# Moving three MLP pieces into a hand-written order list, with one copy moved to GpSimd

## The chip, the cores and the metric

The kernel runs on one core of a Trainium2 chip. The metric is the device time of one execution in microseconds (us), read as the median of several runs. The engines are called PE (matrix products), PEld (loading of weights for PE), DVE (the vector engine), ACT (the scalar engine), POOL (GpSimd) and SP (the engine that issues most transfers). The profiled executions are some 2 us shorter than the timed ones of the same kernel (605.9 us against 607.9). Profiles are therefore compared with profiles and times with times.

## The reference

Eight batches of attention with RMS-normalized queries and keys, then an MLP on a layer norm of the result, with a residual:

```python
q_n, k_n = rmsnorm(q, g_q), rmsnorm(k, g_k)        # q, k, v: (8, 12, 448, 64)
attn = softmax(q_n @ k_n.T / 8)
x = (attn @ v) transposed to (8, 448, 768)
xn = (x - mean(x)) / sqrt(var(x) + 1e-6) * g_ln
out = x + relu(xn @ w_ch1) @ w_ch2                 # w_ch1: 768 x 3072, w_ch2: 3072 x 768
```
(shortened; the softmax and norms are the usual ones)

## The kernel before

The twelve heads of a batch are six pairs. A "unit" is one or two pairs whose queries and keys are normalized together. Batch 0 is emitted in an order written by hand, one token for each piece of work; from then on, the MLP of one batch is interleaved with the attention of the next by arithmetic. The tokens that matter here:

- `S6.0`: scores of pair 6, key block 0, with its exponential on ACT. `V6.0`: its product with the values. `K7`, `Q7`: transposes of the keys and queries of pair 7 on PE, each emptied by a copy on DVE.
- For unit 5: `a5 c5` squares (ACT), `d5 e5` sums (DVE), `g5` root (ACT), `i5 j5` scaling and rounding of the keys (POOL), `k5 l5` two-input operations (DVE), `m5` the doubling of the queries (a copy), `z5` casts of the values (POOL).
- `A N0 N1 N2`: layer norm (DVE), `X0 X1 X2` its transposes, `U0 U1 U2`: the first three of the 24 up products of the MLP, a third of the columns at a time.

```python
POOL_DUP = (1, 2, 4)
ORDER = """
...
V5.3 V5.4 V5.5 Q6 a5 i5 V5.6 T3 T4 S6.0 S6.1 S6.2 S6.3 T5 S6.4 A V6.0 V6.1 N0 V6.2 N1 V6.3
S6.5 S6.6 d5 V6.4 X0 X1 U0 N2 R Q7 X2 c5 e5 j5 g5 k5 l5 z5 U1 U2 V6.5 M m5 V6.6 L7 K7
"""
UP_FIRST = 3
...
def scores(self, p, i):                       # two score banks rotate
    ps = self.ps_s.tile([128, 512], FP32, tag="psS", name="psS")
    nc.tensor.matmul(ps[:, 0:S], c["main"][:, ts(i, 128)], q[:, ts(h, S)], ...)
    nc.scalar.activation(out=c["E"][:, i], in_=ps[:, 0:S], func=AFT.Exp, ...)
...
def mlp_chunks(self, b):                      # a piece: 6 matmuls, and for up products a ReLU on ACT
    def up(f):
        ps = self.ps_m.tile([128, 512], FP32, tag="mlp", name="psH")   # three banks rotate
        ...
        nc.scalar.activation(out=hT[:, f, 0:N], in_=ps[:, 0:N], func=AFT.Relu)
    for f in range(0 if b else UP_FIRST, NFF):
        yield 6 * N / 2.4, (lambda f=f: up(f))
    ...                                       # then the down products, four pieces for each tile
```

The dealer walks through the pieces and, behind each, emits as many "steps" of the next batch's attention as the share of pieces done asks for. A step holds one block of scores, some values, and a part of a unit's preparation. The weights of the second MLP product are loaded in the first such step.

```python
tail = 13
chunks = list(self.mlp_chunks(b))
total = sum(c for c, _ in chunks)
start, goal = self.pos, mark[b + 1]
for i, (cost, emit) in enumerate(chunks):
    ...
    emit()
    done += cost
    upto(int(min(goal, start + (goal - start) * done / (total - 960 * tail))))
```

In batch 0, 44 steps are to be dealt. There are 45 pieces (21 up, 24 down) and the last 13 get none, so 44 steps go over 32 pieces: 1.375 steps a piece.

Of the kernel before, what the change touches and what calls it, by code (L numbers as in the profile page):

```python
# [25 lines left out]
UNIT_PAIR = [PAIR_UNIT.index((u, 0)) for u in range(len(UNITS))]  # L26
EXP_BIAS = -4.0
WARM = 22
DVE_KG, POOL_HI, POOL_DUP, ACT_Q = (0, 1), (1, 2, 3, 4, 5), (1, 2, 4), (0, 1)



# [1 line left out]


ORDER = """
b0 a0 c0 L4 i0 j0 e0 k0 gq0 l0 b1 m0 a1 c1 K0 Q0 d0 G gk0 S0.0 S0.1 d1 e1 L5 i1 g1 j1 l1 k1 m1
z0 b2 a2 S0.2 d2 c2 S0.3 S0.4 K1 V0.0 e2 i2 S0.5 Q1 g2 l2 S0.6 S1.0 j2 V0.1 S1.1 S1.2 m2 b3
V0.2 a3 V0.3 k2 c3 S1.3 K2 V0.4 S1.4 z2 V0.5 Q2 S1.5 V0.6 V1.0 i3 W0 d3 e3 S1.6 V1.1 V1.2 S2.0
j3 T0 V1.3 S2.1 S2.2 Q3 V1.4 S2.3 K3 S2.4 V1.5 V1.6 S2.5 g3 z3 S2.6 V2.0 S3.0 S3.1 V2.1 k3  # L40
S3.2 b4 S3.3 V2.2 l3 a4 V2.3 m3 S3.4 V2.4 K4 S3.5 Q4 V2.5 V2.6 S3.6 Q5 S4.0 V3.0 S4.1 V3.1 i4
V3.2 d4 T1 K5 V3.3 W1 c4 V3.4 V3.5 S4.2 S4.3 V3.6 S4.4 S4.5 W2 e4 V4.0 V4.1 j4 S4.6 S5.0 k4
S5.1 g4 V4.2 l4 S5.2 V4.3 V4.4 V4.5 S5.3 K6 V4.6 z4 V5.0 S5.4 m4 b5 V5.1 G2 S5.5 L6 V5.2 S5.6
V5.3 V5.4 V5.5 Q6 a5 i5 V5.6 T3 T4 S6.0 S6.1 S6.2 S6.3 T5 S6.4 A V6.0 V6.1 N0 V6.2 N1 V6.3
S6.5 S6.6 d5 V6.4 X0 X1 U0 N2 R Q7 X2 c5 e5 j5 g5 k5 l5 z5 U1 U2 V6.5 M m5 V6.6 L7 K7
""".split()
DMA_UNIT = 8
PE_SET = (DMA_UNIT + 1) % 2
# [27 lines left out]
class _Fast:  # L76


    def __init__(self, ctx, tc, sh, q, k, v, gs, g_ln, w1, w2, out):
        self.gs, self.g_ln = gs, g_ln  # L80
        self.tc, self.nc, self.sh = tc, tc.nc, sh
        self.q, self.k, self.v, self.w1, self.w2, self.out = q, k, v, w1, w2, out
        nc = tc.nc
        pool = lambda name, bufs, **kw: ctx.enter_context(tc.tile_pool(name=name, bufs=bufs, **kw))
        self.p_in = pool("p_in", 2)
        self.p_n = pool("p_n", 2)
        self.p_e = pool("p_e", 2)
        self.p_x = pool("p_x", 2)
        self.p_xl = pool("p_xl", 2)
        self.p_m = pool("p_m", 1)  # L90
        self.fix = pool("fix", 1)
        self.ps_tr = pool("ps_tr", 1, space=PSUM)
        self.ps_s = pool("ps_s", 2, space=PSUM)
        self.ps_o = pool("ps_o", 1, space=PSUM)
        self.ps_m = pool("ps_m", 3, space=PSUM)
        fix = self.fix
        self.kU = [fix.tile([128, 1920], FP16, name=f"kU{i}", tag=f"kU{i}") for i in range(2)]
        self.qU = [fix.tile([128, 2, 2, S], FP16, name=f"qU{i}", tag=f"qU{i}") for i in range(2)]
        self.v16 = fix.tile([128, 6, 2, 3, D + 1], FP16, name="v16", tag="v16")
        self.vl = fix.tile([128, 6, 2, D + 1], FP16, name="vl", tag="vl")  # L100
        nc.vector.memset(self.v16[:, :, :, :, D], 1.0)
        nc.vector.memset(self.vl, 0.0)
        nc.vector.memset(self.vl[0:64, :, 0, D], 1.0)
        nc.vector.memset(self.vl[64:128, :, 1, D], 1.0)
        self.rec = fix.tile([128, B * NPAIR, 4, 2], FP32, name="rec_all", tag="rec_all")
        nc.vector.memset(self.rec, 0.01)
        self.rr = fix.tile([128, 7 * B * NPAIR], FP32, name="rr_all", tag="rr_all")
        self.rs = fix.tile([128, B, 4], FP32, name="rs_all", tag="rs_all")
        nc.vector.memset(self.rs, RS_LO)
        self.hT = fix.tile([128, NFF, 512], FP16, name="hT", tag="hT")  # L110
        self.tr = self.ps_tr.tile([128, 1024], FP16, name="tr", tag="tr")
        nc.vector.memset(self.tr[:, 64:128].bitcast(FP32), 0.0)
        self.zero_left(DMA_UNIT)
        self.xs, self.xls, self.st = {}, {}, {}
        self.units, self.loads, self.prs = {}, {}, {}
        self.late, self.preps = [], {}

    def zero_left(self, u):

# [293 lines left out]
    def first_attention(self):  # L413
        nc, gln = self.nc, self.sh.gln
        self.batch(0)
        self.load_first()
        nc.scalar.add_instruction(mybir.InstLoadActFuncSet(
            name=nc.get_next_instruction_name(), act_func_set_id=LN_EXP_SET))
        nc.scalar.activation(self.sh.warm, self.sh.ones, AFT.Ln)
        ln = {}  # L420
        for x in ORDER:
            key, n = x[0], x[1:]
            if x == "S6.0":
                self.batch(1)
            if key == "L":
                self.load_unit(int(n))
            elif x == "G":
                nc.sync.dma_start(gln, self.g_ln.unsqueeze(0).broadcast_to([128, DM]))
            elif x == "G2":
                nc.gpsimd.tensor_scalar(out=gln, in0=gln, scalar1=XS, scalar2=None, op0=ALU.mult)  # L430
            elif key == "W":
                c = int(n)
                self.load_w1(1024 * c, 1024 * c + 1024) if c < 3 else self.load_w2(c - 3)
            elif key in "SV":
                (self.scores if key == "S" else self.values)(*map(int, n.split(".")))
            elif key in "KQT":
                dict(K=self.trans_k, Q=self.trans_q, T=self.stats)[key](int(n))
            elif key in "ANXR":
                ln = ln or self.ln_ops(0)
                ln[x]()  # L440
            elif key == "M":
                gmax = self.sh.gmax
                nc.vector.tensor_reduce(out=gmax, in_=self.sh.gprod, axis=AX.X, op=ALU.max,
                                        apply_absolute_value=True)
                nc.vector.tensor_scalar(out=gmax, in0=gmax, scalar1=1.0 / K_MAX, scalar2=None,
                                        op0=ALU.mult)
            elif key == "U":
                self.up_first(int(n))
            elif key == "H":
                ps = self.ps_m.tile([128, 512], FP32, tag="mlp", name="psW")  # L450
                for _ in range(int(n)):
                    nc.tensor.matmul(ps[:, 0:384], self.sh.id16,
                                     self.v16.rearrange("p s h j d -> p (s h j d)")[:, 0:384],
                                     start=True, stop=True)
            else:
                self.prep_ops(int(x[-1]))[x[:-1]]()
# [228 lines left out]
    def upto(self, target):  # L685
        while self.pos < min(target, len(self.steps)):
            for call in self.steps[self.pos]:
                call()
            self.pos += 1
# [8 lines left out]
    def run_rest(self):  # L698
        steps, mark, upto = self.steps, self.mark, self.upto
        tail = 13  # L700
        for b in range(B):
            chunks = list(self.mlp_chunks(b))
            total = sum(c for c, _ in chunks)
            if b + 1 == B:
                for i, (_, emit) in enumerate(chunks):
                    emit()
                    if i == 2:
                        self.flag()
                break
            start, goal = self.pos, mark[b + 1]  # L710
            done, items = 0.0, None
            for i, (cost, emit) in enumerate(chunks):
                if items and len(chunks) - i <= len(items):
                    items.pop(0)()
# [3 lines that stand above are left out]
                if self.pos >= goal and items is None:  # L718
                    items = self.ln_list(b + 1)
                    items.pop(0)()  # L720
            for op in items:
                op()
            if b + 2 == B:
                upto(len(steps))
# [212 lines left out]
```

## Time and profile before

| | |
|---|---|
| time, median of 3 | 607.91 us (607.86 to 608.15) |
| PE busy | 578.3 of 605.9 us |
| first score | 11.27 us |
| first layer norm transpose (X0) | 49.73 us |
| list and three dealt pieces done, first dealt score (S7.0) | 60.93 us |
| first up product of batch 1 | 121.18 us |

The last rows are milestones read off the PE instructions in order of time. A change in the order list can act only before the last of them: from there to the end, PE is full and takes the same time in every kernel of this study (484.6 to 485.0 us). In the views below, a row of stages has the stretch and its length, then the busy us and number of instructions of PE, PEld, DVE, ACT and POOL, then the granted PE clock and two columns on transfers. A row in order of time has start, duration, engine, line, operation, output from input and, in brackets, the idle time before it and what ended it. Line numbers move by three between the kernels.

### The profile page before, as it was taken

The numbers are of one execution on the slowest core, as the hardware profiler recorded it, in microseconds if no ns is written. First come the engines' busy times: TensorE is split into PE (matmuls) and PEld (weight loads), VectorE is DVE, ScalarE is ACT, GpSimd is POOL, SyncE is SP. The second block draws the span as 40 slices with busy tenths as digits, with TensorE's granted clock in tenths as the row PEclk, the third lists the DMA queues.
The fourth block names the chain that finished last, engine by engine and source line by source line (L and its number), as shares of the span: only waits on it lengthen the run. The fifth ranks groups of instructions, "written<-read, shape, count | busy, mean of one in ns | idle before, by whom it ended". The sixth has DMA issues, their size and how long they took to land.

```text
span 605.9 us, 11525 instructions
## 1 busy us (share of the span) xinstructions
PE 578.3 (95%) x4500; PEld 344.6 (57%) x4500; DVE 286.5 (47%) x618; ACT 360.7 (60%) x697; POOL 189.5 (31%) x245
## 2 busy tenths in 40 slices
PE   2877999999999999999999999999999999999995
PEld 1555666655566666655566666655566666654564
DVE  5799567734346256715256255734256322540011
ACT  6996986278752697358753598548754477124200
POOL 3853432233551355332542345423512000000000
PEclk9999999999999999999999999999999999999998
DMA  9999999479864586844944585847722330130011
GB/s 208 266 213 217 215 224 178 123 195 87 143 157 117 98 129 146 177 135 83 150 121 113 123 125 128 197 116 121 133 65 70 92 62 2 34 98 0 1 53 57
DMA packets 130861, 75.29 MB, mean 124 GB/s; under 512 B 96656, under 2 KB 121040, under 8 KB 130800
## 3 DMA queue, kind: packets, MB, share of 16 engines
q1 hardware_dynamic: 114048, 45.12, 38.3%
q0 software_dynamic: 16080, 28.94, 21.6%
q8 instruction: 37, 0.61, 0.4%
q10 hardware_dynamic: 672, 0.43, 0.2%
q14 instruction: 24, 0.20, 0.1%
HBM read 52.36 MB, written 11.01 MB: 105 GB/s over the span
## 4 chain that ended last, share of the span: by engine, by line
PE 88%; DVE 1%; ACT 1%; issue 0%
PE psC L637 36%; PE psH L621 34%; PE psS L352 8%; PE oA L381 5%; PE oB L383 2%; PE psS L356 1%; PE psS L355 1%; PE tr L330 0%; PE tr L316 0%; ACT E L358 0%; DVE x L398 0%; DVE qn L67 0%; DVE khl L240 0%; ACT khl L215 0%; ACT hT L623 0%
## 5 line engine op out<-in xcount | busy, mean ns | idle before, releaser
L621 PE MATMUL psH<-xnT,w 128*128 128x512 f16 (+1 forms) x1134 | 241.9, 353 | 0.0
L358 ACT ACTIVATE E<-psS,rr_all 128x448 f16<-128x448 f32 x336 | 207.0, 634 | 48.3 <-PE psS L352 43.0
L637 PE MATMUL psC<-w,hT 128*128 128x384 f16 (+1 forms) x1368 | 234.7, 323 | 0.0
L623 ACT ACTIVATE hT<-psH 128x512 f16<-128x512 f32 (+1 forms) x189 | 104.0, 550 | 123.9 <-PE psH L621 121.9
L637 PEld LDWEIGHTS <-hT 128*128 128x128 f16 x1368 | 127.5, 98 | 74.6
L621 PEld LDWEIGHTS <-w 128*128 128x128 f16 x1134 | 102.5, 98 | 80.9 <-issue 0.3
L352 PE MATMUL psS<-qU,kU 128*128 128x448 f16 x288 | 100.6, 357 | 8.3 <-ACT E L358 6.0
L381 PEld LDWEIGHTS <-E 128*128 128x128 f16 x1008 | 70.7, 98 | 49.1 <-issue 4.4
L229 POOL TENSOR_TENSOR qkv<-qkv,gprod 128x896 f32<-128x896 f32 x21 | 43.7, 2081 | 95.8 <-issue 49.5
L381 PE MATMUL oA<-v,E 128*128 128x65 f16 x864 | 66.7, 194 | 0.1
L641 DVE SCALAR_TENSOR_TENSOR x<-psC,rs_all,x 128x384 f32<-128x384 f32 x48 | 29.0, 616 | 71.5 <-PE psC L637 71.1
L396 DVE RECIPROCAL rec_all<-oA 128x6 f32<-128x6 f32 x48 | 9.3, 194 | 94.4 <-PE oA L381 94.2
L383 PE MATMUL oB<-v,E 128*128 128x65 f16 x288 | 51.9, 194 | 0.1
L127 POOL DMA_DIRECT2D qkv<-in_k_dram x14 | 11.2, 798 | 129.7 <-DVE qn L279 61.8
L218 DVE TENSOR_REDUCE ssq<-khl 128x14 f32<-128x896 f32 (+1 forms) x24 | 25.6, 1065 | 44.6 <-ACT khl L215 44.5
L352 PEld LDWEIGHTS <-kU 128*128 128x128 f16 x288 | 28.0, 98 | 25.5 <-issue 6.0
L218 DVE TENSOR_REDUCE ssq<-qn 128x14 f32<-128x896 f32 (+1 forms) x25 | 26.2, 1047 | 21.8 <-ACT qn L215 21.7
L67 DVE SCALAR_TENSOR_TENSOR qn<-qkv,rq 128x256 f16<-128x256 f32 (+1 forms) x72 | 26.3, 425 | 15.1 <-ACT rq L223 15.0
L383 PEld LDWEIGHTS <-E 128*128 128x128 f16 x336 | 32.5, 97 | 0.3 <-DVE xl L403 0.2
L240 DVE TENSOR_TENSOR khl<-qkv,khl 128x896 f16<-128x896 f32 x21 | 22.8, 1088 | 10.8 <-ACT khl L237 7.1
L398 DVE TENSOR_TENSOR x<-oA,rec_all 128x384 f32<-128x384 f32 x48 | 26.8, 558 | 1.5
L545 DVE BATCH_NORM_STATS2 stat<-x 128x6 f32<-128x256 f32 (+1 forms) x75 | 26.2, 404 | 0.6
(104 smaller groups left out, 447.7 us busy)
## 6 DMA issues: line engine op xcount, KB each, us to landing
out_dram<-x SPq DMA_DIRECT2D x20, 384.0 KB, 2.5
qkv<-in_k_dram POOLq DMA_DIRECT2D x14, 384.0 KB, 3.9
qkv<-in_q_dram POOLq DMA_DIRECT2D x14, 384.0 KB, 5.2
qkv<-in_v_dram POOLq DMA_DIRECT2D x14, 384.0 KB, 6.6
w<-in_moe_w_ch_dram POOLq DMA_DIRECT2D x3, 1536.0 KB, 14.6
w<-in_moe_w_ch_dram POOLq DMA_DIRECT2D x2, 2304.0 KB, 24.3
qkv<-in_k_dram SPq DMA_DIRECT2D x7, 384.0 KB, 5.7
qkv<-in_q_dram SPq DMA_DIRECT2D x7, 384.0 KB, 4.6
```

The source lines that it names most:

```text
L67: nc.vector.scalar_tensor_tensor(out=out, in0=x, scalar=8.0, in1=r.unsqueeze(2).broadcast_to([x.shape[0], g, D]), op0=ALU.mult, op1=ALU.mult)
L218: nc.vector.tensor_reduce(out=c["ssq"][:, n], in_=c["sq", n], axis=AX.X, op=ALU.add)
L229: (nc.vector if u in DVE_KG else nc.gpsimd).tensor_tensor(out=c["t"][1], in0=c["t"][1], in1=sh.gprod.unsqueeze(1).broadcast_to([128, g, D] ...
L352: nc.tensor.matmul(ps[:, 0:S], c["main"][:, ts(i, 128)], q[:, ts(h, S)], start=True, stop=True)
L358: nc.scalar.activation(out=c["E"][:, i], in_=ps[:, 0:S], func=AFT.Exp, scale=self.rr[:, g:g + 1], bias=EXP_BIAS)
L381: nc.tensor.matmul(oA[:, t, cs], E[:, i, ts(t, 128)], rhs, start=(i == 0 and t == 0), stop=(i == 6 and t == 2))
L383: nc.tensor.matmul(oB[:, cs], E[:, i, 320:448], rhs, start=(i == 0), stop=(i == 6))
L398: nc.vector.tensor_tensor(out=x[:, :, 128 * hp:128 * hp + 128].rearrange("p t (e d) -> p t e d", e=2), in0=oA[:, :, :, 0:D], in1=rec[:, 0: ...
L621: nc.tensor.matmul(ps[:, 0:N], sh.w1[:, dc, ts(f, 128)], xnT[:, dc, 0:N], start=(dc == 0), stop=(dc == NDC - 1))
L623: nc.scalar.activation(out=hT[:, f, 0:N], in_=ps[:, 0:N], func=AFT.Relu)
L637: nc.tensor.matmul(ps[:, 0:g[1]], hT[:, f, ts(t, 128)], sh.w2[:, f, cols], start=(f == 0), stop=(f == NFF - 1))
L641: nc.vector.scalar_tensor_tensor(out=x[:, cols], in0=ps[:, 0:g[1]], scalar=self.rs[:, b, t:t + 1], in1=x[:, cols], op0=ALU.mult, op1=ALU.add)
```

## The change

The intent: less waiting of PE at the end of the list. Three MLP pieces, which the dealer used to emit, now stand in the list between the last values of pair 6 and the end of unit 5's preparation, to fill PE while DVE finishes K7. Q6 and Q7 go earlier, X2 is freed from Q7, and `m5` leaves DVE for POOL.

```diff
-DVE_KG, POOL_HI, POOL_DUP, ACT_Q = (0, 1), (1, 2, 3, 4, 5), (1, 2, 4), (0, 1)
+DVE_KG, POOL_HI, POOL_DUP, ACT_Q = (0, 1), (1, 2, 3, 4, 5), (1, 2, 4, 5), (0, 1)
 ORDER = """
 ... (the earlier lines are reordered too; cut)
-V5.3 V5.4 V5.5 Q6 a5 i5 V5.6 T3 T4 S6.0 S6.1 S6.2 S6.3 T5 S6.4 A V6.0 V6.1 N0 V6.2 N1 V6.3
-S6.5 S6.6 d5 V6.4 X0 X1 U0 N2 R Q7 X2 c5 e5 j5 g5 k5 l5 z5 U1 U2 V6.5 M m5 V6.6 L7 K7
+S5.6 Q6 V5.3 V5.4 V5.5 a5 V5.6 Q7 S6.0 T4 S6.1 T3 V6.0 S6.2 i5 S6.3 T5 S6.4 A V6.1 N0 N1 V6.2
+N2 V6.3 S6.5 S6.6 d5 V6.4 X0 X1 U0 X2 c5 e5 g5 j5 l5 z5 U1 U2 C k5 V6.5 V6.6 C M R K7 m5 L7 C
 """
...
+            elif key == "C":
+                self.chunks = self.chunks or self.mlp_chunks(0)
+                next(self.chunks)[1]()
...
-            chunks = list(self.mlp_chunks(b))
+            chunks = list(self.mlp_chunks(b) if b else self.chunks)
```

The last line: the pieces that the list has taken are gone from the dealer's list, so its `total` is smaller.

More of the change, by code (lines that the diff above doesn't have):

```diff
@@ L28 @@
 WARM = 22
-DVE_KG, POOL_HI, POOL_DUP, ACT_Q = (0, 1), (1, 2, 3, 4, 5), (1, 2, 4), (0, 1)
+DVE_KG, POOL_HI, POOL_DUP, ACT_Q = (0, 1), (1, 2, 3, 4, 5), (1, 2, 4, 5), (0, 1)
 ORDER = """
-b0 a0 c0 L4 i0 j0 e0 k0 gq0 l0 b1 m0 a1 c1 K0 Q0 d0 G gk0 S0.0 S0.1 d1 e1 L5 i1 g1 j1 l1 k1 m1
-z0 b2 a2 S0.2 d2 c2 S0.3 S0.4 K1 V0.0 e2 i2 S0.5 Q1 g2 l2 S0.6 S1.0 j2 V0.1 S1.1 S1.2 m2 b3
-V0.2 a3 V0.3 k2 c3 S1.3 K2 V0.4 S1.4 z2 V0.5 Q2 S1.5 V0.6 V1.0 i3 W0 d3 e3 S1.6 V1.1 V1.2 S2.0
-j3 T0 V1.3 S2.1 S2.2 Q3 V1.4 S2.3 K3 S2.4 V1.5 V1.6 S2.5 g3 z3 S2.6 V2.0 S3.0 S3.1 V2.1 k3
-S3.2 b4 S3.3 V2.2 l3 a4 V2.3 m3 S3.4 V2.4 K4 S3.5 Q4 V2.5 V2.6 S3.6 Q5 S4.0 V3.0 S4.1 V3.1 i4
-V3.2 d4 T1 K5 V3.3 W1 c4 V3.4 V3.5 S4.2 S4.3 V3.6 S4.4 S4.5 W2 e4 V4.0 V4.1 j4 S4.6 S5.0 k4
-S5.1 g4 V4.2 l4 S5.2 V4.3 V4.4 V4.5 S5.3 K6 V4.6 z4 V5.0 S5.4 m4 b5 V5.1 G2 S5.5 L6 V5.2 S5.6
-V5.3 V5.4 V5.5 Q6 a5 i5 V5.6 T3 T4 S6.0 S6.1 S6.2 S6.3 T5 S6.4 A V6.0 V6.1 N0 V6.2 N1 V6.3
-S6.5 S6.6 d5 V6.4 X0 X1 U0 N2 R Q7 X2 c5 e5 j5 g5 k5 l5 z5 U1 U2 V6.5 M m5 V6.6 L7 K7
+b0 L4 a0 i0 c0 j0 e0 k0 gq0 l0 m0 b1 c1 d0 G a1 K0 Q0 d1 gk0 e1 L5 i1 g1 S0.0 j1 l1 z0 k1 S0.1
+m1 b2 a2 S0.2 d2 V0.0 c2 S0.3 K1 e2 S0.4 i2 Q1 S0.5 g2 l2 S0.6 V0.1 j2 S1.0 V0.2 S1.1 S1.2 b3
+m2 V0.3 k2 z2 c3 V0.4 S1.3 K2 S1.4 a3 S1.5 i3 V0.5 Q2 V0.6 V1.0 V1.1 d3 e3 S1.6 V1.2 S2.0 W0
+V1.3 S2.1 Q3 V1.4 S2.2 K3 S2.3 j3 V1.5 S2.4 g3 T0 V1.6 S2.5 V2.0 S2.6 S3.0 S3.1 z3 V2.1 k3
+S3.2 b4 S3.3 a4 i4 l3 V2.2 V2.3 m3 S3.4 V2.4 K4 S3.5 Q4 V2.5 V2.6 S3.6 V3.0 c4 V3.1 Q5 S4.0
+S4.1 V3.2 d4 V3.3 T1 W1 K5 W2 V3.4 j4 S4.2 S4.3 V3.5 V3.6 S4.4 S4.5 S4.6 e4 V4.0 V4.1 S5.0
+S5.1 k4 g4 V4.2 S5.2 l4 V4.3 V4.4 V4.5 S5.3 K6 V4.6 z4 V5.0 S5.4 S5.5 m4 L6 b5 V5.1 G2 V5.2
+S5.6 Q6 V5.3 V5.4 V5.5 a5 V5.6 Q7 S6.0 T4 S6.1 T3 V6.0 S6.2 i5 S6.3 T5 S6.4 A V6.1 N0 N1 V6.2
+N2 V6.3 S6.5 S6.6 d5 V6.4 X0 X1 U0 X2 c5 e5 g5 j5 l5 z5 U1 U2 C k5 V6.5 V6.6 C M R K7 m5 L7 C
 """.split()
@@ L115, in __init__ @@
         self.units, self.loads, self.prs = {}, {}, {}
-        self.late, self.preps = [], {}
+        self.late, self.preps, self.chunks = [], {}, None
     def zero_left(self, u):
```

## The prediction

> **What bounds the kernel now.** I read the page first (TensorE, PE, is busy 578.3 us of a 605.9 us span, so all its idle time is 27.6 us), then the busy time of each engine by stage, cut where the hand-written order list (attention of batch 0 and its layer norm, up to about 61 us) ends and where the rest begins. Columns: stretch, its length, then busy us (instructions) of PE, weight loads, DVE, ACT, POOL.
>
> ```profile
> 0.00:12.00 12.00, 2.52 (x16) 1.69 (x17) 7.05 (x20) 6.11 (x13) 3.30 (x10) 1.00 0.85 200
> 12.00:45.00 33.00, 25.59 (x299) 16.52 (x298) 27.95 (x50) 31.27 (x62) 22.20 (x26) 1.00 1.05 240
> 45.00:61.00 16.00, 11.96 (x142) 8.43 (x141) 14.60 (x36) 11.09 (x25) 6.55 (x7) 1.00 0.99 220
> 61.00:109.00 48.00, 47.83 (x450) 31.53 (x451) 30.79 (x58) 39.34 (x77) 15.77 (x15) 1.00 1.12 197
> 109.00:595.00 486.00, 485.76 (x3547) 282.24 (x3546) 204.66 (x454) 272.85 (x523) 141.70 (x190) 1.00 0.52 106
> ```
>
> From 61 us to 595 us PE has 0.4 us of idle time. So the time is: the moment at which PE becomes solid, plus PE work that no order changes. From 12 to 45 us ACT is busy 31.3 of 33 us, and DVE has almost no gap after 24 us: those two are the pace, not PE. From 45 to 61 us DVE is busy 14.6 of 16 us and PE waits 4 us. The change can act only there: 4 us in the last stage, a little in the first two.
>
> Then the PE instructions of that last stage, in order of time (start, duration, operation; in brackets the idle time before it and what ended it):
>
> ```profile
> 49.73 0.34 PE L600 MATMUL tr<-id,xn 128*128 128x128 f16 x3 [0.44 <-DVE xn L566]
> 51.19 0.51 PE L600 MATMUL psX<-id,xn 128*128 128x128 f16 x6 [0.59 <-DVE xn L566]
> 54.26 0.49 PE L600 MATMUL tr<-id,xn 128*128 128x128 f16 x6 [0.79 <-DVE qU L335]
> 54.59 2.17 PE L667 MATMUL psU<-xnT,w 128*128 128x128 f16 x36
> 57.38 3.08 PE L621 MATMUL psH<-xnT,w 128*128 128x384 f16 x18
> 60.93 0.55 PE L352 MATMUL psS<-qU,kU 128*128 128x448 f16 x2 [0.46 <-DVE kU L318]
> ```
>
> The third line is the one to see: the last layer norm transpose (X2) uses the one transpose bank that Q7 used just before, so it waits for DVE to empty Q7 (0.79 us), although its own input was ready. The last line: after three MLP pieces (18 matmuls, 3.08 us) PE waits 0.46 us for K7's evacuation. That evacuation stands at the end of a full DVE queue:
>
> ```profile
> 46.54 2.24 DVE L545 BATCH_NORM_STATS2 stat<-x 128x6 f32<-128x256 f32 x9
> 52.05 1.01 DVE L566 SCALAR_TENSOR_TENSOR xn<-x,stat,gln 128x768 f16<-128x768 f32 x1
> 53.58 0.62 DVE L335 COPY qU<-tr 128x896 f16<-128x896 f16 x1 [0.52 <-PE tr L330]
> 54.79 0.56 DVE L608 COPY xnT<-tr 128x768 f16<-128x768 f16 x1 [0.59 <-PE tr L600]
> 55.27 1.08 DVE L218 TENSOR_REDUCE ssq<-qn 128x14 f32<-128x896 f32 x1
> 58.58 0.38 DVE L279 COPY qn<-qn 128x896 f16<-128x896 f16 x1
> 60.21 0.66 DVE L318 COPY kU<-tr 128x960 f16<-128x960 f16 x1
> ```
>
> On ACT, the evacuations of the first three up products stand behind unit 5's root, which waits for a DVE sum:
>
> ```profile
> 56.38 0.23 ACT L221 ACTIVATE rt<-ssq 128x28 f32<-128x28 f32 x1 [2.65 <-DVE ssq L218]
> 56.86 1.23 ACT L671 ACTIVATE hT<-psU 128x384 f16<-128x384 f32 x3
> ```
>
> **What the Trainium skill says.** "Perfetto Trace Analysis", section "Optimization Strategy", says that kernels have regimes with different most-contended engines and that interleaving them may help. The trace agrees that there are such regimes (ACT and DVE before 61 us, PE after). The same page, section "Matmuls", wants independent matmul groups to rotate through PSUM banks so that emptying one overlaps the next; here three banks rotate, and moving a piece ahead means asking when its bank is free. "GPSIMD Engine Reference", section "4.1 Engine selection", calls one-input elementwise work on GpSimd roughly line rate. The trace differs:
>
> ```profile
> L279 DVE COPY qn<-qn x22: 291/394/395, 9.0 to 480.9; 128x896 f16<-128x896 f16 x21, 128x448 f16<-128x448 f16 x1
> L279 POOL COPY qn<-qn x3: 887/931/1661, 14.1 to 42.6; 128x896 f16<-128x896 f16 x2, 128x448 f16<-128x448 f16 x1
> ```
>
> The doubling of a whole unit takes 0.39 us on DVE and 0.93 or 1.66 us on GpSimd. "SBUF — State Buffer", section "Who interferes with whom", explains two sizes: GpSimd shares a port pair with DVE and the later one blocks. The 1.66 us copy, at 20.6 us, lay beside a two-input DVE subtraction (k2); the 0.93 us one, at 42.6 us, began as another was ending.
>
> **The change part by part.** I compared the old and new list engine by engine. No work is added or dropped on PE, ACT or DVE except that m5 leaves DVE for GpSimd; the rest is order.
>
> (1) Q6 goes before V5.3 and Q7 behind V5.6, out of the layer norm stage. DVE can then empty Q6 at about 44.4 us instead of idling 0.30 us until 44.68; so the evacuation of V5.6 starts about 0.3 us earlier, at 44.9 us, and ends at 46.25. Q7's copy (0.54 us from start to next start) is now in front of the statistics: they run 46.8 to 48.95, the aggregate to 49.35, the three norms (about 1.0 us each) to 50.35, 51.3 and 52.3. d5 (1.0 us) now follows the last norm, to 53.3. So the first transpose comes some 0.2 us later than before, the second at 51.35 (51.19 before), the third norm 0.75 us earlier (52.3 against 53.06).
>
> (2) PE: X1 51.35 to 51.7; U0's first 12 matmuls to 52.35; its last 6 wait for the bank of X1 until about 52.65, as they did (0.22 us before). X2 runs at 53.0 instead of 54.26, with Q7's 0.4 us of PE work gone into an earlier gap. Its copy on DVE 53.5 to 54.05. U1 and U2 (2 x 1.0 us) end at 55.35, where they ended at 56.6.
>
> (3) The MLP pieces now follow directly: C. But the first needs the bank of the first up product, whose evacuation stands on ACT behind g5, which needs e5 on DVE: 54.05 to 55.05, root to 55.6, evacuation to 56.05. PE waits about 0.7 us: a new wait. Then piece 56.1 to 57.05, V6.5 and V6.6 (0.35), piece to 58.4, K7 (0.4), piece to 59.8.
>
> (4) K7's wait (0.46 us). DVE: l5 from 55.5 (0.45 us of waiting for the root that k5 filled before), k5 to 57.5, V6.6's evacuation (1.3) and M (0.3) to 59.2, K7's copy to 59.8. The rest of the program is dealt out by shares of the pieces left; with three fewer left, working the program's step arithmetic by hand gives two further pieces before S7.0 (about 61.8 us), so K7 is in time and the wait is gone.
>
> (5) m5 on GpSimd: 0.30 us less DVE work before K7, 0.9 to 1.7 us on an engine that has 9 idle us in that stage; ready by 58.5 us, needed by Q8 after 65 us. Worth nothing alone.
>
> At the same amount of PE work before stood at 60.93 us and the new order stands at 59.8: a gain of 1.1 us. (6) At the start, c1 goes ahead of a1 although unit 1's q lands after its k: ACT waited 0.23 us for q at 9.67; now a1 (0.58) waits behind it, and Q0's copy comes about 0.45 us later; g1 now precedes S0.0, so l1 comes about 0.9 us earlier. By S0.3 I find ACT 0.2 us behind, and g2, which paces DVE, at 19.0 instead of 18.9. After that DVE is full with the same work, so I carry 0.1 us. Sum: -1.1 + 0.1, and 0.1 for the risk below: -0.9 us.
>
> **The rivals.** (a) A late transfer. The first half of the second MLP weights is loaded in the first dealt-out step, behind a6 on ACT and a multiplication on GpSimd. It was issued at 62.04 us:
>
> ```profile
> w<-in_moe_w_ch_dram POOLq DMA_DIRECT2D x1, 2304.0 KB, 23.4
> ```
>
> so it landed near 85.4, and the first down product began at 90.2. Now that step comes after the sixth piece instead of the third: a6 near 61.5, issue near 64.4, landing near 87.8 (an estimate, with the same 23.4 us). The down products should start near 88.7. Margin 0.9 instead of 4.8 us. If the queue is slower, PE waits up to 1.5 us and the gain is eaten: about 608. (b) DVE takes it back: Q7's copy before the statistics and the new wait for g5 grow, and only the 0.46 us go: 607.4. Speaks for it: DVE is 91% busy there. Against: the order gives 0.75 us on the third norm by plain subtraction. (c) The early reordering is worth more than I find: ACT waits 1.0 us and DVE 4 us between 12 and 24 us; if half of that were won, 605.9. Against: ACT's own work from 5.9 to 44.5 us leaves 2.3 us of gaps in all, and the new start adds one.
>
> **Range and chances.** 607.91 - 0.9 = 607.0 us. Range 605.8 to 608.1: below, (c) and a full 1.1; above, (a). 2% is 12 us; all idle time before 61 us is 21 us, of which 8.5 is the first load, so faster by 2% gets 0.01, slower 0.01, within 2% 0.98.
>
> **What would show it.** Right: X2 without a wait for Q7; a wait of 0.4 to 1 us at the first moved piece, ended by ACT; no wait for K7; S7.0 after five pieces; m5 at 0.9 to 1.7 us on GpSimd; PE solid from about 57 us; the first stages within 0.4 us of before at V5.6. Wrong: idle PE before the first down product near 89 us (a); norms ending later than 53 us (b); V5.6 over 0.6 us earlier or later (c).

## The result and the profile after

| | before | after |
|---|---|---|
| median of 6 runs each, same rounds | 608.07 us (607.86 to 609.48) | 608.95 us (608.59 to 609.14) |
| profiled span | 605.9 us | 607.2 us |
| first score | 11.27 | 11.70 |
| first score to X0 | 38.46 | 38.94 |
| X0 to first up product of batch 1 | 71.45 | 71.93 |
| rest | 484.72 | 484.63 |

The ratio of the two is 1.001, with a 95% interval of 0.9997 to 1.0023: the same within 2%, and rather slower than faster. A ratio here is the mean time of one kernel's fast runs over the mean of the other's fast runs of the same rounds, so it is not quite the ratio of the medians. The predicted 607.0 us and the range to 608.1 us were missed on the high side.

The stages of the changed kernel, as in the prediction's first view:

```profile
12.00:45.00 33.00, 25.77 (x296) 16.69 (x294) 27.51 (x50) 30.72 (x62) 22.22 (x26) 1.00 1.07 240
45.00:61.00 16.00, 12.58 (x150) 8.87 (x147) 14.62 (x34) 10.54 (x24) 7.06 (x7) 1.00 0.95 211
61.00:109.00 48.00, 46.80 (x436) 30.62 (x434) 30.11 (x56) 39.52 (x78) 15.64 (x14) 1.00 1.08 196
109.00:595.00 486.00, 485.76 (x3553) 282.82 (x3552) 205.84 (x456) 274.22 (x525) 143.04 (x190) 1.00 0.52 106
```

From 45 to 61 us PE is busy 12.58 us instead of 11.96: the change did there what it was made for. The third row is the surprise. PE was busy for 47.83 of these 48 us; now it is 46.80. Its instructions in order of time, some rows picked, show both:

```profile
53.83 0.50 PE L603 MATMUL tr<-id,xn 128*128 128x128 f16 x6
...
57.02 1.14 PE L624 MATMUL psH<-xnT,w 128*128 128x384 f16 x6 [0.68 <-ACT hT L674]
...
62.63 0.35 PE L352 MATMUL psS<-qU,kU 128*128 128x448 f16 x1
...
65.89 0.35 PE L352 MATMUL psS<-qU,kU 128*128 128x448 f16 x1 [0.17 <-ACT E L358]
...
67.63 0.35 PE L352 MATMUL psS<-qU,kU 128*128 128x448 f16 x1 [0.42 <-ACT E L358]
...
79.81 0.35 PE L352 MATMUL psS<-qU,kU 128*128 128x448 f16 x1 [0.46 <-ACT E L358]
```

X2 no longer waits, the first moved piece waits 0.68 us for its bank, and S7.0 follows without a wait: as predicted. The last three lines are new. A score waits until an exponential has emptied one of the two score banks. Before, the whole stretch from 61 us on had one such wait, of 0.2 us.

The brackets understate the loss, because the ends of matmuls are modelled. Taken from start to start, less the usual spacing of such matmuls, the breaks between 61 and 110 us are 0.33, 0.57 and 0.16 us near 66 to 70 us, 0.62 us at 79.81, and 0.24 us twice at 83.4 and 84.0: some 2 us, where the page's busy time shows 1.2. In the kernel before there are two breaks over 0.15 us in the same count: 0.63 us at K7 and 0.34 us at 66.04. One of the breaks after is not ACT's: the one at 84.0 us stands before a transpose of queries, and DVE had emptied K from the transpose bank only at 83.95 us.

A second reading needs no such sum. Before, PE had done the list and three pieces when S7.0 began at 60.93 us; 60.25 us later came the first up product of batch 1. After, the same PE work, the list with its three pieces, was done at 60.68 us (two more pieces follow before S7.0), and the first up product of batch 1 came 61.89 us later. So the list ended 0.25 us earlier, and 1.64 us were lost behind it.

Why ACT holds PE there shows in ACT's own order. Before:

```profile
58.94 0.94 ACT L215 ACTIVATE khl<-qkv 128x896 f32<-128x896 f32 x1
...
60.89 0.94 ACT L215 ACTIVATE qn<-qkv 128x896 f32<-128x896 f32 x1
...
63.13 0.97 ACT L237 ACTIVATE khl<-qkv 128x896 f16<-128x896 f32 x1
```

After:

```profile
62.25 0.94 ACT L215 ACTIVATE khl<-qkv 128x896 f32<-128x896 f32 x1
...
63.46 0.95 ACT L215 ACTIVATE qn<-qkv 128x896 f32<-128x896 f32 x1
64.30 0.63 ACT L358 ACTIVATE E<-psS,rr_all 128x448 f16<-128x448 f32 x1
...
66.07 0.98 ACT L237 ACTIVATE khl<-qkv 128x896 f16<-128x896 f32 x1
66.91 0.67 ACT L358 ACTIVATE E<-psS,rr_all 128x448 f16<-128x448 f32 x1
```

These are the two squares and the rounding of the keys of unit 6, each nearly 1 us, which is longer than an exponential (0.63 us). Before, the first square ran under the three dealt pieces, when no scores were due. After, those pieces lie in the list and have nothing of unit 6 beside them, and squares, rounding and exponentials come in one crowd. From the first square to the start of the rounding it was 4.19 us and is now 3.82. The stage view of ACT around it:

```profile
65.00:70.00 5.00, 4.41 (x34) 2.64 (x33) 4.09 (x5) 4.97 (x13) 4.79 (x5) 1.00 0.70 114
...
75.00:80.00 5.00, 4.54 (x41) 2.86 (x40) 2.97 (x7) 4.73 (x10) 2.37 (x2) 1.00 1.24 222
```

The same stretches before:

```profile
65.00:70.00 5.00, 4.83 (x41) 2.98 (x40) 2.27 (x4) 4.63 (x13) 1.58 (x2) 1.00 1.25 213
...
75.00:80.00 5.00, 5.00 (x48) 3.33 (x47) 4.67 (x11) 5.00 (x11) 4.63 (x5) 1.00 1.24 220
```

So a full ACT alone does not stop PE (5.00 against 5.00 before, at 75 to 80 us); it does when a long operation stands in front of the exponential whose bank PE needs next.

The arithmetic of the dealer says why the crowd is there. With 42 pieces left and the same 13 left without a step, 44 steps go over 29 pieces instead of 32: 1.52 steps a piece instead of 1.375. And the first step stands behind the seventh up product instead of the fourth, so unit 6's preparation and the scores of pair 7 begin together:

| behind up product (counted from 0) | before | after |
|---|---|---|
| 3 | b6 a6 i6, weights | (in the list) |
| 4 | d6 | (in the list) |
| 5 | c6, S7.0, e6, S7.1 | (in the list) |
| 6 | j6, S7.2, K8 | b6 a6 i6, weights |
| 7 | g6 v6, S7.3 | d6, c6, S7.0 |
| 8 | | e6, S7.1 |
| 9 | | j6, S7.2, K8, g6 v6, S7.3 |

(steps worked out from the code; values left out)

Two more lines answer to the prediction: `m5` on POOL, and the weights.

```profile
57.75 1.66 POOL L279 COPY qn<-qn 128x896 f16<-128x896 f16 x1 [1.33 <-DVE qn L67]
...
65.30 1.50 POOL L523 DMA_DIRECT2D w<-in_moe_w_ch_dram  x1
```

The weights are issued at 65.30 us and take 20.4 us, so they land at 85.7; the first down product starts at 90.92 without a wait.

### The profile page after: what moved, and what is told of

Its sections match the earlier page's. It is cut to its first block, busy times and chain, and to the rows that moved or that the text cites. A ratio compares the mean times of both kernels' runs of the same rounds, so it can differ in the third digit from the quotient of the medians.

```text
span 607.2 us, 11525 instructions
## 1 busy us (share of the span) xinstructions
PE 579.0 (95%) x4500; PEld 345.6 (57%) x4500; DVE 286.2 (47%) x617; ACT 360.8 (59%) x697; POOL 191.3 (32%) x246
## 4 chain that ended last, share of the span: by engine, by line
PE 85%; DMA 2%; ACT 1%; DVE 1%; SPq 0%; issue 0%; ACTq 0%
PE psC L640 36%; PE psH L624 33%; PE psS L352 7%; PE oA L381 5%; DMA qkv<-in_q_dram 2%; PE oB L383 2%; PE psS L355 1%; PE psS L356 1%; DMA qkv<-in_k_dram 0%; ACT E L358 0%; PE tr L330 0%; ACT hT L626 0%; ACT khl L215 0%; SPq L135 0%; DVE khl L240 0%
## 5 line engine op out<-in xcount | busy, mean ns | idle before, releaser
L127 POOL DMA_DIRECT2D qkv<-in_k_dram x14 | 11.2, 799 | 129.5 <-DVE qn L279 61.8
```

## The experiments

The theory to test, called A in the expectations: the loss comes from the dealer. The three pieces are gone from its list, so the steps come later and denser, and ACT, not DVE, stops PE. Its rivals were that the new list itself is the cost (the reordered beginning, Q7's copy before the statistics), that the moved pieces cost through the bank that waits for a ReLU, and that nothing more than the variation of the first load is seen. Where the texts use another letter, it is a rival that the same text names.

The timed differences are near the limit of what five rounds settle (the intervals are about 0.13% or 0.8 us to either side). The stage lengths of the profiles are finer, from X0 on, and carry the argument; the times are given beside them. Each stage length comes from one profiled execution. All kernels gave correct results. The kernels were timed in three calls, against the same kernel before: medians 608.48, 608.26 and 608.27 us.

| kernel | median us | ratio, 95% interval | X0 to first up product of batch 1 |
|---|---|---|---|
| before | see above | 1 | 71.45 |
| order_only | 608.03 | 0.9997, 0.9983 to 1.0010 | 70.34 |
| pieces_only | 609.25 | 1.0015, 1.0001 to 1.0028 | 72.45 |
| same_density | 609.17 | 1.0014, 1.0000 to 1.0027 | 72.12 |
| casts_gpsimd | 608.87 | 1.0009, 0.9996 to 1.0023 | 71.70 |
| deal_as_before | 608.65 | 0.9998, 0.9984 to 1.0012 | 70.96 |
| tail_only | 608.49 | 1.0000, 0.9984 to 1.0015 | 70.72 |
| unit6_early | 614.75 | 1.0107, 1.0090 to 1.0124 | 76.68 |
| relu_first | 614.91 | 1.0106, 1.0091 to 1.0122 | 77.28 |
| unit6_list | 609.41 | 1.0017, 1.0004 to 1.0029 | 72.11 |
| k7_first | 608.81 | 1.0006, 0.9994 to 1.0018 | 72.76 |
| k7_first_old | 609.01 | 1.0015, 1.0002 to 1.0028 | 72.18 |
| after_again | 609.25 | 1.0021, 1.0008 to 1.0034 | 71.93 |

### The new list without the pieces

```diff
-U1 U2 C k5 V6.5 V6.6 C M R K7 m5 L7 C
+U1 U2 k5 V6.5 V6.6 M R K7 m5 L7
-            chunks = list(self.mlp_chunks(b) if b else self.chunks)
+            chunks = list(self.mlp_chunks(b))
```

> The new list without the three moved pieces: all 45 pieces of batch 0 are dealt out with the steps as in the kernel before; m5 stays on GpSimd. Theory A (the loss is made after 61 us, because three fewer pieces push the first dealt-out steps three pieces later and pack the rest denser, so that ACT falls behind and PE waits for exponentials): the stretch from 61 to 109 us is as tight as before (idle PE under 0.3 us), the list's own saving of about 0.7 us stays, 607.0 to 607.8 us. Theory B (the early part of the new order is what costs; the first squares of the changed kernel's profile came 0.5 us late): the time stays within 0.4 us of the changed kernel, 608.6 to 609.3 us.

The wait for K7 is back, and it is the last one; from 61 us on PE is full (PE in order of time, then the stage):

```profile
60.57 0.55 PE L352 MATMUL psS<-qU,kU 128*128 128x448 f16 x2 [0.89 <-DVE kU L318]
```

```profile
61.00:109.00 48.00, 47.99 (x452) 31.79 (x451) 30.89 (x60) 38.75 (x77) 14.64 (x15) 1.00 1.14 197
```

From X0 on this kernel is 1.11 us shorter than before and 1.59 us shorter than the full change. Of the 1.11 us, 0.84 lie in front of S7.0 (10.36 us after X0 instead of 11.20), although K7 is waited for longer. So the new end of the list is worth something from X0 on, and the moved pieces with their dealing lose more than that. The time, 608.03 us, lies between what A expected (607.0 to 607.8) and what B expected (608.6 to 609.3).

### The old list with the three pieces at its end

```diff
-S6.5 ... U1 U2 V6.5 M m5 V6.6 L7 K7
+S6.5 ... U1 U2 V6.5 M m5 V6.6 L7 K7 C C C
```
(the token C and the shortened dealing as in the change; m5 back on DVE)

> The old list with only the three pieces put at its end, after K7, and m5 back on VectorE: on PE the same pieces in the same place as before, but the dealing starts behind them. Theory A: the loss appears alone: the 0.46 us wait for K7 goes, some 1.5 to 2 us of waiting for exponentials between 62 and 85 us come, 608.8 to 609.8 us. Theory B: nothing but the K7 wait changes, 607.4 to 607.9 us.

This is almost the same instruction order for PE as before, up to S7.0: the pieces that the dealer emitted behind K7 are now written there. What differs is the dealing. PE in order of time:

```profile
67.62 0.35 PE L352 MATMUL psS<-qU,kU 128*128 128x448 f16 x1 [0.42 <-ACT E L358]
...
79.80 0.35 PE L352 MATMUL psS<-qU,kU 128*128 128x448 f16 x1 [0.46 <-ACT E L358]
```

The waits of the full change stand at the same places (67.63 and 79.81 us there), and the kernel is 1.00 us longer than before from X0. The loss needs neither the new list nor `m5` on POOL.

### The change with the old dealing

```diff
             start, goal = self.pos, mark[b + 1]
             done, items = 0.0, None
+            if b == 0:
+                done, total = 2880.0, total + 2880.0
+                upto(int(goal * done / (total - 960 * tail)))
```

> The changed kernel, pieces still in the list, but the three pieces counted in the dealing: the four steps that the old kernel deals out behind its first three pieces now stand directly behind the list, and every later step follows the same piece as in the kernel before. Theory A (dealing, not the moving itself): the stretch from the list to the solid block of down products is as long as in the kernel before, the extra waits at 65 to 70 us and 80 to 84 us go except for about 0.3 us where the four steps come at once and K7 is just in time; 1.3 to 1.7 us below the changed kernel, 607.2 to 608.0 us where before is 608.4. Rival (the moved pieces themselves hold banks or ACT so that the scores starve): the waits at 65 to 70 us stay, 608.7 to 609.3 us.

The dealer now counts the three pieces of the list as done, so the first four steps are emitted as soon as the list ends and the rest at 1.375 a piece. PE in order of time has two waits for exponentials left, both at unit 6, and none from 74 to 86 us:

```profile
63.39 0.35 PE L352 MATMUL psS<-qU,kU 128*128 128x448 f16 x1 [0.31 <-ACT E L358]
...
67.02 0.35 PE L352 MATMUL psS<-qU,kU 128*128 128x448 f16 x1 [0.17 <-ACT E L358]
```

From X0 it takes 70.96 us against 71.93 for the change. The list with its pieces is done 10.03 us after X0 here and 10.04 us in the change, so 0.97 of the 1.64 us lost behind the list come back although the same pieces stand at the same places. What remains shows as the waits at unit 6, whose first four steps now come at once. The time, 608.65 us, missed the 607.2 to 608.0 us that A expected. This is the closest test of the cause: the pieces stay and only the dealing differs.

### The change with the old density alone

```diff
-                upto(int(min(goal, start + (goal - start) * done / (total - 960 * tail))))
+                upto(int(min(goal, start + (goal - start) * done / (total - 960 * (tail if b else 10)))))
```

> The changed kernel with the tail of batch 0 cut from 13 pieces to 10, so that steps per piece are as in the kernel before (44 steps over 32 pieces), only three pieces later. Theory A with density as the cause: the waits for exponentials after 65 us shrink to under 0.4 us in sum, but the layer norm of batch 1 has 3 pieces less to hide under and may show up to 2 us at about 120 us. Theory A with the late start as the cause (unit 6's squares and cast fall together with the first exponentials whatever the density): the waits near 65 to 70 us stay at about 1 us. Theory B: no change in 61 to 109 us.

44 steps over 32 pieces again, but beginning three pieces later than before. The waits at unit 7 are gone. The one at unit 6 stays, and a new one comes at the end of the stage (PE in order of time):

```profile
65.29 0.35 PE L352 MATMUL psS<-qU,kU 128*128 128x448 f16 x1 [0.59 <-ACT E L358]
...
122.34 1.46 PE L624 MATMUL psH<-xnT,w 128*128 128x512 f16 x6 [1.14 <-DMA xnT<-xn]
```

With only ten pieces behind the last step, the transposes of batch 1's layer norm are no longer covered. The late start is what crowds unit 6, the density is what crowds unit 7, and the tail of 13 pieces cannot simply be cut: all told it is no faster than the change (72.12 against 71.93 us).

### Less work on ACT

```diff
-DVE_KG, POOL_HI, POOL_DUP, ACT_Q = (0, 1), (1, 2, 3, 4, 5), (1, 2, 4, 5), (0, 1)
+DVE_KG, POOL_HI, POOL_DUP, ACT_Q = (0, 1), (1, 2, 3, 4, 5, 6, 7), (1, 2, 4, 5), (0, 1)
```

> The changed kernel with the key casts of units 6 and 7 on GpSimd instead of ACT, two ACT instructions of 0.84 us less in the crowded stretch. Theory A (ACT is the engine that falls behind): most of the 1.9 us of lost PE time between 61 and 90 us comes back, 607.2 to 608.0 us. Rival C (the waits come from the later loads of units 7 and 8, which show in the chain of waits as a 10.6 us transfer of queries): no gain, 608.6 to 609.3 us, or slower because GpSimd delays the cast behind the issue of the weights.

The rounding of the keys of units 6 and 7, 0.98 us each, goes from ACT to POOL. The wait at 67.6 us is gone, those at 65.9 and 79 us stay, and a new one appears:

```profile
79.05 0.35 PE L352 MATMUL psS<-qU,kU 128*128 128x448 f16 x1 [0.45 <-ACT E L358]
...
83.76 0.22 PE L327 MATMUL tr<-id,qn 128*128 128x128 f16 x1 [0.84 <-DVE kU L318]
```

On DVE a copy of K now stands behind unit 7's queries (1.48 us). Of the 1.9 us, most of which was expected back, 0.23 us came, measured from X0. The time, 608.87 us, lies in the range of rival C. The change's own trace speaks against C all the same: from 60 to 91 us none of the idle time of ACT or DVE was ended by a transfer. That the wait behind the rounding goes when the rounding leaves ACT agrees with A; as a remedy it only passes the wait to DVE.

### The new end of the list alone

```diff
 (the list of before up to V5.1, then)
+V5.1 G2 S5.5 L6 V5.2 S5.6 Q6 V5.3 ... U1 U2 k5 V6.5 V6.6 M R K7 m5 L7
```
(old dealing, no pieces in the list)

> The old list up to V5.1 and the new one after it (Q6 and Q7 before the layer norm, norms before d5, m5 on GpSimd), without moved pieces. It divides the gain of the new order without pieces between its early part and its tail. My prediction's sum for the tail (the first scores of pair 6 to S7.0) was 1.1 us with the pieces; without them K7's wait stays at about 0.9 us, so 0.3 to 0.6 us. If the early part is neutral, this run is within 0.3 us of the new order without pieces, and first score to first layer norm transpose is 38.9 us in both; if the early part costs, it is 38.5 here.

K7's wait is 0.88 us, X0 to the first up product of batch 1 is 70.72 us: 0.73 us better than before, where order_only was 1.11 us better. The time is that of before (ratio 1.0000), because X0 came 39.41 us after the first score instead of 38.46. That is neither of the two lengths expected (38.9 or 38.5). The start of V5.6 on PE, the last values of pair 5, divides it into two parts, over all 14 profiles:

| us | old end of the list (before, pieces_only, k7_first_old) | new end of the list (the other eleven) |
|---|---|---|
| first score to V5.6 | 33.34, 33.36, 34.07 | 32.80 to 33.83 |
| V5.6 to X0 | 5.12 in each | 5.57 to 5.59 |

The first part varies by more than the lists differ in it, so the reordered beginning shows no effect. The second part is a cost of the new end, 0.46 us in every profile: Q7's copy, 0.62 us on DVE, now stands ahead of the statistics, which in the change start 2.38 us after V5.6 and in the kernel before 1.93 us. From V5.6 to the first up product of batch 1, which counts this cost too, it is 76.57 us before, 75.91 in order_only, 76.30 in tail_only, 76.55 in deal_as_before, 77.50 in the change and 77.57 in pieces_only.

### Unit 6 begun in the list

```diff
-U1 U2 C k5 V6.5 V6.6 C M R K7 m5 L7 C
+U1 U2 C k5 m5 b6 a6 i6 W3 V6.5 V6.6 C M R K7 d6 c6 L7 C S7.0 e6 S7.1
```
(W3 is the load of the second weights; the dealer then leaves it out)

> The changed kernel with unit 6's first preparation (both squares, multiplication, both sums, the first half of the second weights) and the first two scores of pair 7 drawn into the list around the three pieces, so that it fills ACT's gaps between 56 and 62 us; what remains is dealt over the remaining pieces at the old density. Theory A: waits for exponentials after 62 us under 0.4 us in sum, K7's evacuation is again waited for by 0.2 to 0.4 us, 607.0 to 607.8 us where before is 608.4. If the squares on ACT delay the pieces' own evacuations, PE waits for banks at the second or third piece and the gain is half.

It failed, for a reason of my own making. POOL in order of time:

```profile
46.68 2.06 POOL L230 TENSOR_TENSOR qkv<-qkv,gprod 128x896 f32<-128x896 f32 x1
59.52 0.83 POOL L286 CAST v<-qkv 128x768 f16<-128x768 f32 x1 [10.77 <-DMA qkv<-in_v_dram]
```

A cast of values stands on POOL ahead of unit 5's rounding of the keys and waits 10.77 us for its transfer. I had left unit 6's casts to the dealer, and in the built program two sets of casts and the rounding of unit 5 come in this changed order. K7 then comes late and PE waits 4.58 us at 66.01 us. Why the casts came first in the built program was not pursued. The run says nothing of theory A.

### As before, and the root behind the ReLUs

```diff
-X2 c5 e5 g5 j5 l5 z5 U1 U2 C k5 V6.5 V6.6 C M R K7 m5 L7 C
+X2 c5 e5 j5 U1 U2 g5 l5 z5 C k5 m5 b6 a6 i6 W3 V6.5 V6.6 C M R K7 d6 c6 L7 C S7.0 e6 S7.1
```

> As the run before it, and unit 5's root (g5) put behind the evacuations of the first three up products on ACT, so that the first moved piece finds its bank free. Theory: the 0.68 us wait at the first moved piece goes; unit 5's chain (root, scaled queries, key remainder, K7's evacuation) comes 0.6 to 0.8 us later, so S7.0 waits for K7 by 0.8 to 1.2 us instead. If both hold, the sum is the same within 0.3 us: then the bound of this stage is the VectorE chain and no order of ACT mends it.

The bank wait of the first piece is gone (X0 to the first moved piece is 5.6 us instead of 6.38), so that cost can be removed, but the same wait on POOL as in unit6_early holds PE for 5.50 us, and then the clock drops as well. The stage from 61 to 70 us of unit6_early and of relu_first:

```profile
61.00:70.00 9.00, 4.42 (x22) 2.17 (x21) 6.11 (x11) 4.71 (x10) 7.49 (x7) 0.81 0.41 107
```

```profile
61.00:70.00 9.00, 3.15 (x15) 1.61 (x15) 6.58 (x12) 3.97 (x7) 8.02 (x9) 0.64 0.38 103
```

The column before the last two is the granted clock, 0.81 and 0.64 where other kernels have 1.00. The Trainium skill, "TensorE: Matmul & The Clock Gate", section "HAM oscillation — how this bites in real kernels", gives as the rule that PE should have no idle gap of more than some 3.4 us; these gaps of 4.58 and 5.50 us agree with it. Inconclusive for A.

### Unit 6 begun in the list, its values too

```diff
-U1 U2 C k5 m5 b6 a6 i6 W3 V6.5 V6.6 C M R K7 d6 c6 L7 C S7.0 e6 S7.1
+U1 U2 C k5 m5 b6 a6 i6 W3 z6 V6.5 V6.6 C M R K7 d6 c6 L7 C S7.0 e6 S7.1
```

> The run with unit 6 prepared early, mended: in it GpSimd had the values of unit 6 put ahead of unit 5's key cast and waited 10.8 us for their transfer; now the list also holds unit 6's value copies behind the weights' transfer, so GpSimd keeps the old order. Theory A (late and dense dealing makes ACT fall behind): the waits for exponentials at 62 to 90 us are under 0.5 us in sum, the pieces' own 0.68 us bank wait stays, K7 is waited for by 0.2 to 0.6 us; 607.2 to 608.2 us where before is 608.3. If the waits are not from dealing, 608.8 to 609.5.

With the casts in the list POOL's order is mended, and the experiment does what unit6_early was for. It is a miss for what I had expected of A. The time is not better (1.0017) and, at 609.41 us, lies in the range for the case that the waits do not come from dealing; and PE still waits for an exponential at unit 6 (PE in order of time):

```profile
63.85 0.35 PE L353 MATMUL psS<-qU,kU 128*128 128x448 f16 x1 [0.94 <-ACT E L359]
```

ACT is busy 8.79 of the 9 us from 61 to 70. Bringing unit 6 forward also brought S7.0 and S7.1 forward, so squares and exponentials still meet: S7.0 ran at 61.38 us, ACT's second square of unit 6 at 61.95, and the first exponentials only at 63.17. An early start is not enough; my reading, which no further run tests, is that the long operations of a unit and the scores have to be apart. Only the kernels with three dealt pieces behind the list, and a wait for K7 behind these, had that, and I found no order that has this with the pieces moved.

### K7 before l5, in the new list and in the old

```diff
 (order_only)
-X2 c5 e5 g5 j5 l5 z5 U1 U2 k5 V6.5 V6.6 M R K7 m5 L7
+X2 c5 e5 g5 j5 k5 z5 U1 U2 V6.5 V6.6 K7 l5 M R m5 L7
 (before)
-X2 c5 e5 j5 g5 k5 l5 z5 U1 U2 V6.5 M m5 V6.6 L7 K7
+X2 c5 e5 j5 g5 k5 z5 U1 U2 V6.5 V6.6 K7 l5 M m5 L7
```

> The new order without moved pieces, and on VectorE unit 5's key remainder (k5), V6.6's evacuation and K7's evacuation go before the scaled queries (l5) and M, which nothing needs until Q8. The 0.9 us wait for K7 before S7.0 goes (K7 ready about 1.9 us earlier, 58.5 us); nothing else moves. First layer norm transpose to the first batch 1 up product 0.8 to 1.0 us shorter than in the new order without pieces (70.3 us there, 71.5 in the kernel before); 606.6 to 607.6 us where before is 608.3.

> The kernel before with that one mending alone (l5, M, m5 behind K7): its 0.63 us wait for K7 goes and nothing else, so 0.5 to 0.7 us below before in the stretch from the first layer norm transpose on, 607.4 to 608.0 us where before is 608.3. If unit 5's queries come late for Q8, a wait there shows at 64 to 66 us.

These ask whether K7's wait can be removed more cheaply, by taking l5 (1.09 us on DVE) and M from in front of its copy and leaving the dealer alone. The wait is gone in both, and neither is faster: 1.0006 and 1.0015. In the first, PE in order of time has

```profile
63.23 0.35 PE L352 MATMUL psS<-qU,kU 128*128 128x448 f16 x1 [0.59 <-ACT E L358]
...
67.11 0.35 PE L352 MATMUL psS<-qU,kU 128*128 128x448 f16 x1 [0.42 <-ACT E L358]
```

and the second has 0.59 us at 63.28 and 0.17 us at 66.92. In the second, S7.0 came 10.57 us after X0 instead of 11.20, and waits for exponentials took that back without any change in the dealing. The first shows less, because its S7.0 is no earlier from X0 than that of order_only (10.44 and 10.36 us), for the reason given below. The times, 608.81 and 609.01 us, missed the expected 606.6 to 607.6 and 607.4 to 608.0. Both also have one wait near 119 us for DVE to empty a down product. In the list of PE's waits of k7_first (us, times, longest) it is

```profile
PE psC L640 <- DVE x L644: 1.0, 1, 1.0
```

and 0.6 us in k7_first_old. I did not find out which earlier order on DVE causes it. The profile of k7_first also had a granted clock of 0.89 from 45 to 61 us (0.50 from 52.5 to 55.5) without a long gap of PE. Its first dealt piece began 7.51 us after X0 and that of order_only 6.38 us, so about 1.1 us of its 72.76 us may be due to the clock; that is a second reason not to compare it closely, and the cause is open.

### The change again

> The changed kernel once more, beside these on one chip. Its stretch from the first layer norm transpose to the first up product of batch 1 is 71.9 us within 0.1 (before: 71.45), with the same five waits between 65 and 84 us; the stretch from the first scores to that transpose is 38.4 to 39.3 us, as it varied among the runs that share this early list. 0.5 to 1.2 us above before.

The changed kernel in the last call, on the runs of before made there: X0 to the first up product of batch 1 is 71.93 us as in the first profile, and the waits of the first profile are there again, 0.2 us later. The stage length repeats to a hundredth. That is one repeat of one kernel, but parts of it repeat as well: X0 to the first moved piece is 6.37 or 6.38 us in all seven profiles in which the pieces stand in the new list behind g5. So differences of 0.5 us are taken as real here. The time is 609.25 us, 0.98 above before (0.5 to 1.2 expected), ratio 1.0021.

### What the twelve runs say together

Leaving out the two spoiled kernels and the two with K7 moved, the kernels fall into two groups. Those with the old dealing (order_only, tail_only, deal_as_before) have ratios of 0.9997 to 1.0000. Those with the pieces in the list and another dealing (pieces_only, same_density, casts_gpsimd, unit6_list, after_again, and the change itself) have 1.0009 to 1.0021. None beats the kernel before by more than the interval, and the intervals of the two groups overlap. The profiles divide in the same way: from V5.6 to the first up product of batch 1, the first group has 75.91 to 76.55 us and the second 77.28 to 77.70, where before has 76.57.

Theory A's expected times fared badly: only pieces_only (608.8 to 609.8) came out inside its range, the gains hoped for from order_only, deal_as_before, casts_gpsimd, unit6_list and the two runs with K7 moved were all missed on the high side. What supports A is where the waits appear and go in the traces.

## Why the prediction was wrong, step by step

What held. X2 ran without a wait at 53.83 us (53.0 predicted; the start was late by part of it). The first moved piece waited 0.68 us, ended by ACT (0.7). K7's wait went, with two more pieces before S7.0 at 62.63 us (61.8). `m5` took 1.66 us (0.9 to 1.7) and nobody waited for it. The third norm ended at 52.9 us (52.3). The weights landed at 85.7 us and were needed at 90.92, so rival (a) did not come.

What was off in size. The third moved piece ended at 60.68 us, not 59.8. The first square in this profile began 0.51 us later than before, as these lines show, before and then after, on ACT in order of time:

```profile
5.85 0.58 ACT L215 ACTIVATE hT<-hT 128x448 f32<-128x448 f32 x1 [1.84 <-DMA hT<-in_k_dram]
```

```profile
6.36 0.58 ACT L215 ACTIVATE hT<-hT 128x448 f32<-128x448 f32 x1 [2.36 <-DMA hT<-in_k_dram]
```

The transfers were issued within 0.1 us of each other. The list of order_only begins as the change's does, and there the square began at 5.45 us; so this is variation of the first load and no part of the change. By V5.6 the change was 0.46 us late, 0.43 of it at the first score. That is about half of the 0.9 us by which the gain at the end of the list fell short. Rival (b), DVE taking some back through Q7's copy, came in part: V5.6 to X0 took 0.45 us longer, where step (1) had put the first transpose "some 0.2 us later". Rival (c), an early gain or loss of over 0.6 us, is not to be seen above the variation; the 1.0 us of waiting that it gives ACT between 12 and 24 us is a misreading, since ACT was busy 11.73 of these 12 us.

The step that failed is the first one: "So the time is: the moment at which PE becomes solid, plus PE work that no order changes", with its consequence in the last part, "PE solid from about 57 us". It was read from a stage of 48 us in which PE was busy 47.83 us. But the order does change what lies behind the list. Step (4) even worked out that the dealing changes, and used it only as help for K7 ("two further pieces before S7.0") and, in rival (a), for the weights. It did not ask what the same three missing pieces do to ACT. The average hid it: ACT was busy 39.34 of 48 us, 82%, which looks like room. In stretches of 5 us it was 4.76 at 60 to 65 us and 5.00 at 75 to 80 us already. The Trainium skill, "Perfetto Trace Analysis", section "Identifying the Most-Contended Engine", takes occupancy as a fair measure for ACT and says that the busy share of matmuls is not a good one for PE. The second half agrees: PE's breaks of some 2 us showed as 1.2 us of idle. The first half needs short stretches to hold here.

In place of that step the runs put a term of +1.6 us behind the list (1.64 us from the milestones). Of it, 0.97 us is the dealing (deal_as_before); for the other 0.7 us there are the waits at unit 6 that deal_as_before still has, and no run removes them with the pieces in the list. Set against the 1.16 us that the new end of the list does give from X0 on (10.04 us instead of 11.20), a loss of about 0.5 us follows, and that is what the profile shows (71.93 against 71.45). With the 0.45 us of Q7's copy in front of X0, 0.93 us of the 1.3 us between the two profiles belong to the change. The other 0.46 us lie in front of V5.6, where kernels with the same list beginning differ by as much.

## What to carry to other kernels

When work is moved out of the reach of a scheduler that deals by shares, everything behind it is dealt anew: work out both orders, and look at every engine that the denser order feeds, in stretches as short as the crowd and not in the average of the stage. An engine that is full without stopping the bound one has no room for a denser order, and long operations ahead of the one that frees a bank are what turns it into a wait. A removed wait is a gain only if the next engine in line has slack there: K7's wait was taken away in three ways here (pieces in the list, K7 ahead of l5 in the old list and in the new), and each time waits for exponentials took its place.

## What the Trainium skill lacked or had wrong

- "Perfetto Trace Analysis", "Identifying the Most-Contended Engine": occupancy of ACT over the stage (39.3 of 48 us, 82%) gave no sign that 5-us stretches inside it were full (5.00 of 5). The page gives no length for the stretch over which to take it. Its caution on the busy share of matmuls holds: some 2 us of breaks showed as 1.2 us of idle.
- "GPSIMD Engine Reference", "4.1 Engine selection": the row calls one-input work roughly line-rate and gives no figure for that rate. The copy of 896 elements in each partition took 0.93 us on POOL at 42.6 us in the kernel before, about 1 ns an element, so the row is not shown to be wrong, as the prediction takes it to be. But the same copy took 0.38 us on DVE, and 1.66 us on POOL while DVE ran its two-input subtraction; one rate does not cover that.
- "TensorE: Matmul & The Clock Gate", "HAM oscillation — how this bites in real kernels": its rule agrees with clocks of 0.81 and 0.64 around gaps of 4.58 and 5.50 us, so nothing is wrong there. In k7_first the clock was 0.50 from 52.5 to 55.5 us without such a gap; the runs leave the cause open.
- No page that I know of gives the spread of a first load: with transfers issued within 0.2 us of each other, the first square began between 5.45 and 6.36 us in the profiles.
